# Two last V tiles cut otherwise, and a result whose halves lie on two partition quadrants of one PSUM bank

## The chip, the cores and the metric

One core of one Trainium2 chip. The metric is the device time of one execution in microseconds (us), as the median of several executions; the profile is of one execution. "Span" is the profile's own length, some 1.8 us shorter than the device time. The rounds of the experiments ran on three chips; each time is compared with the kernel before of the same rounds.

## The reference, cut to what matters

A decode step of a parallel block: attention of 4 batches and 32 heads over a cache of 8192 positions, plus a SwiGLU branch, plus the input. The caches K and V are 268 MB each and are read once.

```python
q = (xn @ wq) ...                                         # B=4, H=32, Dh=128
scores = einsum("bhqd,bhkd->bhqk", q, k_cache) * Dh**-0.5  # Sk = 8192
o = einsum("bhqk,bhkd->bhqd", softmax(scores), v_cache)
return x + o.reshape(B, 1, H*Dh) @ wo + (silu(xn @ w_gate) * (xn @ w_up)) @ w_down   # 4 x 512
```

## The kernel before

K and V come in 64 tiles of 4 MB each (128 partitions of 32 KB, 128 tokens of 128 values), all issued on one queue into five buffers. VectorE turns a K tile in eight transposes, TensorE (PE) multiplies it with q, two tiles later the V tile is multiplied with the weights. The last V tile is handled token by token (`pv_last`), in parts, so that little work is left after the last bytes. The output projection of a head is two matmuls of 256 columns, one for each half of the result, collected in two PSUM banks.

```python
def wo_mm(i):                                  # output projection of head i, summed up in PSUM
    for half in range(2):
        mm(yo_ps[half][0:B, :], otn[:, i, :],
           wo_t[0][:, i * D + half * DH:i * D + (half + 1) * DH], start=False)
# ... (in the loop over tiles)
    load_v(nv, (32, 32, 32, 16, 16) if nv == NT - 1 else (32,) * 4 if nv == NT - 2 else (T,))
# ...
    if npv == NT - 1:                          # the last V tile
        xps = x_tile()
        pv_last(xps, range(T // 2))
        fin_2(H // HT - 1, xps, nb=B - 1, start=False)   # the other three batches
        pv_last(xps, range(T // 2, T))
        fin_3(H // HT - 1, xps)                # divides: otn of the last two heads
# ...
    if bv % 2 == 0:
        row_sums(npv // 2)                     # a PE sum, and a reciprocal on VectorE that waits for it
# ... (after the loop)
res = [persist.tile([B, DH], dt.bfloat16, name=f"res{j}") for j in range(2)]
nc.vector.tensor_copy(out=res[0][:], in_=yo_ps[0][0:B, :])
nc.sync.dma_start(out=out_flat[:, 0:DH], in_=res[0][:])
nc.scalar.copy(out=res[1][:], in_=yo_ps[1][0:B, :])
nc.scalar.dma_start(out=out_flat[:, DH:D], in_=res[1][:])
```

## Time and profile before

| | before |
|---|---|
| device time | 1288.93 us, median of 3 (1288.82 to 1289.40) |
| span | 1287.1 us |
| HBM read | 550.77 MB, 428 GB/s |
| last V part landed | 1282.67 us |
| first of the last 59 P·V matmuls | 1266.04 us |
| from the last store's issue to the end | 2.10 us |

The page gives the shares of the whole span; a change of the tail is read from the chain and the timeline of the last 30 us (start, length, engine, line, operation, and in brackets the idle time before it and what ended that).

```profile
1254.35 0.18 DVE L328 RECIPROCAL rcp<-mps 128x4 f32<-128x4 f32 x1 [8.48 <-PE mps L76]
1254.45 9.11 DVE L277 STREAM_TRANSPOSE kt<-slot 128x1024 uint32<-128x1024 uint32 x8
```

The last K tile landed at 1253.35 by the records, but its transposes stand behind a reciprocal on VectorE that waits for PE.

### The profile page before, as it was taken

How to read it: one execution, taken by the hardware profiler on the slowest of the kernel's cores; microseconds unless marked ns; L12 is line 12 of the kernel's file. 1: busy time of each engine (PE TensorE's matmuls, PEld its weight loads, DVE VectorE, ACT ScalarE, POOL GpSimd, SP SyncE). 2: the span in 40 equal slices, each digit the busy share in tenths (PEclk: the TensorE clock that was granted, in tenths of full speed). 3: DMA queues.
4: the chain of work that ended last, by engine and by line, in shares of the span. 5: the costliest groups of instructions: out<-in, count | busy, mean ns of one | idle time of the engine just before them, and what ended most of it. 6: DMA issues, size and time to landing. Idle time of an engine off the chain costs nothing.

```text
span 1287.1 us, 11189 instructions
## 1 busy us (share of the span) xinstructions
PE 1083.1 (84%) x4778; PEld 430.3 (33%) x4778; DVE 738.1 (57%) x951; ACT 39.7 (3%) x87; POOL 5.3 (0%) x13
## 2 busy tenths in 40 slices
PE   4888888888888798897997888888887988978788
PEld 1334333333333333332333333333333333333334
DVE  6663556546556556466556566465465465573544
ACT  1000000000000000000000000000000000000000
POOL 1000000000000000000000000000000000000000
PEclk9898898998989999898998989989899898989899
DMA  9999999999999999999999999999999999999997
GB/s 407 427 430 435 437 425 437 429 436 431 432 435 428 436 432 433 431 432 435 431 435 428 434 432 431 436 431 433 430 434 431 437 430 432 433 431 427 433 434 304
DMA packets 21529, 551.49 MB, mean 428 GB/s; under 512 B 2268, under 2 KB 2792, under 8 KB 3944
## 3 DMA queue, kind: packets, MB, share of 16 engines
q1 hardware_dynamic: 21464, 550.78, 99.4%
q8 instruction: 37, 0.61, 0.2%
q14 instruction: 12, 0.10, 0.0%
q10 hardware_dynamic: 16, 0.01, 0.0%
HBM read 550.77 MB, written 0.00 MB: 428 GB/s over the span
## 4 chain that ended last, share of the span: by engine, by line
DMA 50%; PE 31%; DVE 14%; issue 5%; ACT 1%; SPq 0%; DVEq 0%
DMA slot<-in_A_k_cache_dram 44%; PE oacc L76 17%; PE sps L76 12%; DVE kt L277 11%; DMA slot<-in_A_v_cache_dram 6%; PE mps L76 1%; DVE ptz L318 1%; DVE o L356 1%; PE xps L76 1%; DVE o_sb L354 1%; ACT o_sb L353 0%; PE mps L299 0%; DVE otn L377 0%; PE yo_ps L76 0%; DVE rcp L328 0%
## 5 line engine op out<-in xcount | busy, mean ns | idle before, releaser
L76 PE MATMUL sps<-kt,zq 128*128 128x512 bf16 x2048 | 578.3, 421 | 145.2 <-DVE kt L277 128.7
L277 DVE STREAM_TRANSPOSE kt<-slot 128x1024 uint32<-128x1024 uint32 x512 | 587.6, 1210 | 90.4 <-DMA slot<-in_A_k_cache_dram 89.5
L76 PE MATMUL oacc<-slot,ptz 128*8 128x512 bf16 x2016 | 450.4, 379 | 0.4 <-DMA slot<-in_A_v_cache_dram 0.4
L76 PEld LDWEIGHTS <-zq 128*128 128x128 bf16 x2048 | 212.0, 104 | 496.1 <-issue 317.0
L76 PEld LDWEIGHTS <-ptz 128*8 128x8 bf16 x2016 | 177.5, 92 | 258.1 <-issue 27.8
L328 DVE RECIPROCAL rcp<-mps 128x4 f32<-128x4 f32 x32 | 5.9, 183 | 281.9 <-PE mps L76 281.9
L354 DVE TENSOR_TENSOR o_sb<-o_sb,rowu 128x512 f32<-128x512 f32 x16 | 11.1, 693 | 89.2 <-ACT o_sb L353 89.0
L76 PE MATMUL xps<-rowy,o 128*32 128x4 f32 (+1 forms) x228 | 13.5, 205 | 37.3 <-DVE o L356 37.3
L293 DVE TENSOR_REDUCE mx<-sps 128x1 f32<-128x512 f32 x32 | 22.1, 692 | 18.5 <-PE sps L76 18.5
L76 PEld LDWEIGHTS xps<-rowy,o 128*32 128x32 f32 (+1 forms) x228 | 12.1, 154 | 44.9 <-DVE o L356 44.9
L268 DVE COPY zq<-qt 32x8 bf16<-32x8 bf16 x128 | 21.3, 166 | 1.3
L302 DVE TENSOR_REDUCE nm<-mps 128x4 f32<-128x64 f32 x32 | 7.2, 225 | 24.0 <-PE mps L299 24.0
L356 DVE TENSOR_REDUCE o<-o_sb 128x128 f32<-128x512 f32 x16 | 16.3, 1020 | 0.5
L76 PEld LDWEIGHTS mps<-rowb,rs 128*128 128x128 f32 x64 | 9.5, 186 | 13.8 <-issue 13.8
L76 PEld LDWEIGHTS <-slot 128*128 128x128 bf16 x272 | 11.7, 126 | 3.5 <-DVE slot L188 2.6
L76 PE MATMUL mps<-rowb,rs 128*128 128x4 f32 x64 | 12.3, 263 | 0.0
L353 ACT COPY o_sb<-oacc 128x512 f32<-128x512 f32 x16 | 9.4, 586 | 76.8 <-PE oacc L76 76.8
L377 DVE TENSOR_TENSOR otn<-xps,rcp 32x16 bf16<-32x16 f32 x28 | 4.8, 170 | 11.7 <-PE xps L76 10.3
L299 PE MATMUL mps<-ident_f,mx 128*128 128x128 f32 x32 | 10.3, 323 | 0.8 <-DVE mx L293 0.8
L299 PEld LDWEIGHTS mps<-ident_f,mx 128*128 128x128 f32 x32 | 4.3, 133 | 14.7 <-DVE mx L293 14.2
L170 PE MATMUL xps<-ident,kt 4*128 4x4 bf16 x4 | 0.3, 173 | 10.1 <-DVE kt L165 10.1
L76 PE MATMUL yo_ps<-slot,otn 128*4 128x256 bf16 x64 | 8.2, 281 | 0.3 <-DVE otn L366 0.3
(150 smaller groups left out, 148.5 us busy)
## 6 DMA issues: line engine op xcount, KB each, us to landing
slot<-in_A_k_cache_dram SPq DMA_DIRECT2D x64, 4096.0 KB, 39.2
slot<-in_A_v_cache_dram SPq DMA_DIRECT2D x62, 4096.0 KB, 36.8
slot<-in_A_v_cache_dram SPq DMA_DIRECT2D x7, 1024.0 KB, 22.3
slot<-in_A_wq_dram SPq DMA_DIRECT2D x1, 4096.0 KB, 12.3
slot<-in_A_wo_dram SPq DMA_DIRECT2D x1, 3584.0 KB, 40.2
slot<-in_B_w_gate_dram SPq DMA_DIRECT2D x1, 1792.0 KB, 31.9
slot<-in_B_w_up_dram SPq DMA_DIRECT2D x1, 1792.0 KB, 35.8
slot<-in_B_w_down_dram SPq DMA_DIRECT2D x1, 1792.0 KB, 30.9
```

Of the source, the lines that this page charges most:

```text
L76: nc.tensor.matmul(out_ap, lhsT=lhsT, rhs=rhs, start=start, stop=True, skip_group_check=True, **kw)
L268: nc.vector.tensor_copy(out=zq[gr % 2][a * QB:(a + 1) * QB, :, :, XO + a * QB].rearrange("p b (j r) -> p r j b", r=2), in_=qt[a * QB:(a + ...
L277: nc.vector.transpose(out=kt[:].bitcast(dt.uint32).rearrange("p (j t r) -> p t j r", j=2, r=QB), in_=src.rearrange("p (t j r) -> p t j r", ...
L293: nc.vector.reduce_max(out=mx[:], in_=s_ps[gr][:], axis=AX.X)
L299: nc.tensor.matmul(mps[:, 0:P], lhsT=nmx.pop(gr)[:, 0:1].to_broadcast([P, P]), rhs=ident_f[:, :], is_transpose=True, start=True, stop=True ...
L302: nc.vector.tensor_reduce(out=nm[:], in_=by_row(mps[:, 0:P]), axis=AX.XY, op=ALU.max, negate=True)
L318: nc.vector.transpose(out=t_[y * HP:(y + 1) * HP, :, y, :, :].rearrange("p s u x -> p s (u x)"), in_=p_[y * HP:(y + 1) * HP, :].rearrange( ...
L328: nc.vector.reciprocal(out=rcp[j][:, :, 2 * bp:2 * bp + 2], in_=mps[:, P:P + B].rearrange("p (y b) -> p y b", y=HT))
L353: nc.scalar.copy(out=o_sb[:].rearrange("p u d -> p (u d)"), in_=o_acc[j % 2][:])
L354: nc.vector.tensor_tensor(out=o_sb[:], in0=o_sb[:], in1=rowu[:].unsqueeze(2).to_broadcast([P, NV, Dh]), op=ALU.mult)
L356: nc.vector.reduce_sum(out=o1[:], in_=o_sb[:].rearrange("p u d -> p d u"), axis=AX.X)
L377: nc.vector.tensor_tensor(out=otn[q0:q1, blk * 4:blk * 4 + 4, :], in0=xps[q0:q1], in1=r_[q0:q1, y, :].unsqueeze(1).to_broadcast([QB, 4, B] ...
```

## The change

The intent: let the two matmuls of a head run side by side (each half of the result on its own partition quadrant), share the rounding between two engines, and leave 8 tokens, not 16, to multiply after the last landing.

```diff
-    psY = ... bufs=2                      +    psY = ... bufs=1
-    yo_ps = [psY.tile([B, DH], dt.float32, name="yo_ps") for _ in range(2)]
+    yo_ps = psY.tile([2 * QB, DH], dt.float32, name="yo_ps")          # QB = 32
+    nc.vector.memset(yo_ps[:], 0.0)
+    def yo_mm(lhsT, rhs, start):
+        for a in range(2):
+            mm(yo_ps[a * QB:a * QB + B, :], lhsT, rhs[:, a * DH:(a + 1) * DH], start=start)
 ...
-            load_v(nv, (32, 32, 32, 16, 16) if nv == NT - 1 else (32,) * 4 if nv == NT - 2 else (T,))
+            load_v(nv, (64, 32, 16, 8, 8) if nv == NT - 1 else (64, 64) if nv == NT - 2 else (T,))
 ...
-    (the two roundings and two stores shown above)
+    res = persist.tile([2 * QB, DH], dt.bfloat16, name="res")
+    nc.scalar.copy(out=res[:, DH // 2:DH], in_=yo_ps[:, DH // 2:DH])
+    nc.vector.tensor_copy(out=res[:, 0:DH // 2], in_=yo_ps[:, 0:DH // 2])
+    nc.sync.dma_start(out=out_flat[:, 0:DH], in_=res[0:B, :])
+    nc.scalar.dma_start(out=out_flat[:, DH:D], in_=res[QB:QB + B, :])
```

(The two other users of `yo_ps` call `yo_mm`.)

## The prediction

> **What bounds the kernel now.** I read the page first: slices, the chain that ended last, the DMA issues. Then I read the stretch after 1270 us by windows, the chain again in order of time, the timeline, and when each transfer was issued and landed. Lines of the page:
>
> ```profile
> span 1287.1 us, 11189 instructions
> PE 1083.1 (84%) x4778; PEld 430.3 (33%) x4778; DVE 738.1 (57%) x951; ACT 39.7 (3%) x87; POOL 5.3 (0%) x13
> DMA  9999999999999999999999999999999999999997
> HBM read 550.77 MB, written 0.00 MB: 428 GB/s over the span
> ```
>
> The DMA row is 9 in every slice but the last: the kernel streams 551 MB of K and V and nothing else matters as long as the stream never pauses. The packet records say the same: a 32 KB packet takes 1213 ns nearly everywhere, one behind the other, and I found no pause after the first microseconds. So a change can only win in the head, in the stream's length, or in what follows the last landing. This one touches the tail and one memset in the head. Windows of the tail (us, busy of PE, PEld, DVE, ACT, POOL, granted clock, DMA share, GB/s):
>
> ```profile
> 1270.00:1275.00 5.00, 5.00 (x29) 2.17 (x28) 0.00 (x0) 0.00 (x0) 0.00 (x0) 1.00 1.00 418
> 1275.00:1277.00 2.00, 2.00 (x11) 0.83 (x10) 0.00 (x0) 0.00 (x0) 0.00 (x0) 1.00 0.57 242
> 1279.00:1281.00 2.00, 1.51 (x52) 1.42 (x49) 1.48 (x2) 0.00 (x0) 0.00 (x0) 1.00 0.51 203
> 1281.00:1283.00 2.00, 1.52 (x57) 1.43 (x54) 0.00 (x0) 0.00 (x0) 0.00 (x0) 0.56 0.14 55
> ```
>
> From 1275 us about half of the DMA capacity is idle: some of the 16 engines have finished, the slower ones work through the last parts until about 1282.4. The chain in order of time (start, length, what):
>
> ```profile
> 1265.54 17.13 DMA slot<-in_A_v_cache_dram
> 1282.67 0.05 issue
> 1282.71 0.60 PE xps L76 x16
> 1283.34 0.18 DVE otn L366
> 1283.56 1.03 PE yo_ps L76 x4
> 1284.61 0.36 ACT res L458
> ```
>
> So the last V part lands at 1282.67. Sixteen small matmuls, the division, four output matmuls and one rounding follow, then the stores:
>
> ```profile
> 1280.81 1.42 PE L76 MATMUL xps<-ptz,slot 128*128 128x2 bf16 x48
> 1284.40 0.41 DVE L456 CAST res<-yo_ps 4x256 bf16<-4x256 f32 x1 [0.89 <-PE yo_ps L76]
> 1284.84 0.35 SPq L457 DMA_DIRECT2D out_dram<-res  x1
> 1285.00 0.28 ACTq L459 DMA_DIRECT2D out_dram<-res  x1
> ```
>
> From the last store's issue at 1285.00 to the end at 1287.10 are 2.10 us; from the last V landing to the end, 4.43 us. That is all this change can work on, 0.34% of the span, so 2% is out of reach unless it starts a stall.
>
> **What the Trainium skill says.** "TensorE: Matmul & The Clock Gate", section "Part 3: Packing small matmuls", says that matmuls on different tiles of the array run at the same time. The trace agrees: in the head, 32 query matmuls of 512 columns over four column strips took 3.61 us, so 0.11 us each, where the same shape into one strip (the P·V matmuls, in the tail 59 in 12.06 us) takes 0.20 us at twice the granted clock. "PSUM — Partial Sum Buffer", section "PSUM bank collisions raise a hardware error", says that two engines may not access one bank in one quadrant at once, not even two reads. The trace of before has no such pair; the changed program, where both roundings read both quadrants, does, and its instruction list orders them. "VectorE: DVE Perf Modes", section "The TRN2 errata", gives a PSUM copy 172 + N cycles at 1.2 GHz on ScalarE and 120 + N at 0.96 GHz on VectorE: 357 and 392 ns for N = 256; the trace has 362 and 412. "DMA: Bandwidth & Descriptors", section "Anatomy of one DMA", puts a DMA's fixed cost at about 2.0 us, mostly the receipt; the 2.10 us here fits, and the change leaves it.
>
> **The change part by part.**
>
> *Parts of the last two V tiles.* Before: four parts of 32 tokens, then 32, 32, 32, 16, 16. After: 64 and 64, then 64, 32, 16, 8, 8: seven transfers for nine. An engine's share of a part is 8 packets, one per partition. The packet records give 159 ns for 4 KB, 309 for 8 KB, 535 for 14 KB, 1213 for 32 KB: some 8 ns and 0.0368 ns per byte, so (estimates) 610 ns for 16 KB and 83 for 2 KB, less 3 ns of overlap each. Both tiles cost an engine 8 x (7 x 306 + 2 x 156) = 19.63 us before and 8 x (3 x 607 + 306 + 156 + 2 x 80) = 19.54 after: -0.09 us.
>
> What remains after the last landing: 8 tokens, not 16. 16 took 0.60 us; with a step of 0.028 us (0.60 less a latency of 0.17, over 15) 8 take 0.36: -0.23 us. This holds only if PE is there in time. It restarts at 1280.70, after the sum of the other three batches, and did 48 tokens in 1.42 us, so it is through token 119 near 1282.4, or a little after the fourth part (about 1282.0); the fifth lands at 1282.58. It waits, with 0.2 us to spare.
>
> *Output matmuls.* The halves go to partitions 0 to 3 and 32 to 35 of one bank, two column strips, so the two matmuls of a head can run side by side. Before: four in a row in 1.03 us. At the granted half clock 256 columns take 0.213 us (half of the 0.427 in which four 512-column matmuls passed in the head), and 1.03 - 3 x 0.213 = 0.39 is the first one's latency. After: 0.39 + 0.213 = 0.61: -0.42 us. The 60 earlier output matmuls also pair up, inside the stream, where it is worth nothing.
>
> *Rounding.* Both engines now take 128 of the 256 columns, on 64 partitions, so each instruction is shorter: by the formulas, shifted to what the trace has, 0.25 us on ScalarE and 0.28 on VectorE. But the built program makes VectorE's copy wait for ScalarE's: they are not side by side. And both stores need both copies. Before: last matmul to last store's issue 1285.00 - 1284.59 = 0.41 us. After: 0.02 + 0.25 + 0.04 + 0.28 + 0.03 = 0.62: +0.21 us. Run truly side by side they would give 0.33, so the ordering costs about 0.3 of the possible gain.
>
> *Head.* One memset of 64x256 on VectorE: half of the 485 ns of a 128x512 one, 0.25 us. It falls before a 1.68 us wait of VectorE for the first K tile. Nothing.
>
> Sum: -0.09 - 0.23 - 0.42 + 0.21 = -0.53 us. 1288.93 - 0.53 = 1288.4.
>
> **The rivals.**
> 1. *A coarse part starves PE.* Two parts of 64 land later than the first of four. In the records the first 32-token part landed at 1265.52; at 8 x 0.306 = 2.45 us a part, the halves land near 1267.9 and 1272.8. PE reaches that tile 27 matmuls of 0.204 us after 1266.04, at 1271.5, and its second half at 1274.8. The last tile's first 64 tokens land near 1277.7 (the records have 1277.76 for their second half), and PE wants them at 1278.16. Margins of 2.0 and 0.4 us. If I misjudge the second, the delay partly hides behind the 1280.57 restart; I give a loss above 0.3 us a 10% chance.
> 2. *The stream ends at another time.* In before, the last two issues waited for a transfer slot (1263.05 and 1265.54). After, only one waits, for a K load that landed at 1253.35. But no engine ran dry before, so nothing is won. If the slow engines' lag came out differently, the end could move by a microsecond either way; this, like the run-to-run spread of 1288.82 to 1289.40, is larger than what I predict, and makes most of the range.
> 3. *The column strips do not overlap* for four-row results. Then 0.42 us is lost and the change is about -0.1: 1288.8. The query matmuls speak against it.
> 4. *The two roundings run together.* Then -0.8: 1288.1. The wait in the built program speaks against it.
>
> **Range and chances.** Rivals 3 and 4 span 1288.1 to 1288.8; the spread and rival 2 add some 0.6 us either way: 1287.4 to 1289.2. Beyond 2% (26 us) nothing I can name reaches; faster 0.5%, slower 1% for a stall I have overlooked, same 98.5%.
>
> **What would show it.** The page should look the same but for the tail. Right: a last landing within 0.3 us of 1282.6, then 8 matmuls in about 0.36 us; four output matmuls in about 0.6; ScalarE's copy at 0.25 us, and VectorE's beginning only when it ends, at 0.28; both stores issued within 0.1 us of each other, some 3.9 us or less between landing and end. Wrong: four output matmuls still near 1.0 us; copies that overlap; PE waiting for V before 1278, or arriving after the last landing; a landing more than 0.5 us away from 1282.6, which would mean that the stream and not the tail made the difference.

## The result, and the profile after

| | before | after |
|---|---|---|
| device time, median (range, runs) | 1288.91 (1288.78 to 1289.40, 6) | 1289.18 (1288.56 to 1289.31, 6) |
| span of the profiled execution | 1287.1 | 1287.4 |
| ratio | | 1.0001, 95% interval 0.9988 to 1.0014 |

A ratio is the mean time of one kernel's runs over that of the other's of the same rounds, so not quite the ratio of the medians. Kernels are compared only within the same rounds. The time lies inside the predicted range, at its upper edge; the half microsecond of gain that was forecast is not there. The chain of the changed kernel in order of time:

```profile
1266.74 12.00 PE oacc L76 x59
...
1280.11 1.04 DVE o L361
1281.15 0.04 issue
1281.19 2.31 PE xps L76 x66
1283.51 0.02 issue
1283.53 0.18 DVE otn L371
1283.71 0.04 issue
1283.75 0.61 PE yo_ps L76 x4
1284.36 0.02 issue
1284.38 0.27 ACT res L461
1284.65 0.02 issue
1284.67 0.28 DVE res L462
```

Where the chain of before went through the landing of the last V part, this one has no transfer at all in its last 20 us: P·V matmuls, the sum of the other batches, 64 tokens in one go, the output. The timeline says the same of those 64 tokens: no wait in brackets.

```profile
1281.64 1.85 PE L76 MATMUL xps<-ptz,slot 128*128 128x2 bf16 x64
1283.75 0.59 PE L76 MATMUL yo_ps<-slot,otn 128*4 128x256 bf16 x4 [0.26 <-DVE otn L371]
1284.67 0.28 DVE L462 CAST res<-yo_ps 64x128 bf16<-64x128 f32 x1 [0.98 <-ACT res L461]
1284.98 0.35 SPq L463 DMA_DIRECT2D out_dram<-res  x1
1284.99 0.28 ACTq L464 DMA_DIRECT2D out_dram<-res  x1
```

The last V part had landed at 1282.47, when PE still had some 35 tokens to go. Term by term, from the two profiles:

| stretch | before | after | difference |
|---|---|---|---|
| start to the end of the last token matmul | 1283.30 | 1283.49 | +0.19 |
| division, to the first output matmul | 0.26 | 0.26 | 0 |
| output matmuls (with the step to the rounding left out) | 1.01 | 0.59 | -0.42 |
| last output matmul to the last store's issue | 0.43 | 0.65 | +0.22 |
| last store's issue to the end | 2.11 | 2.38 | +0.27 |
| sum (span) | 1287.11 | 1287.37 | +0.26 |

Two terms are as predicted. Two are not: the token matmuls end later and not earlier, and the close is 0.27 us longer.

### The profile page after: what moved, and what is told of

It is laid out like the page before. It is cut to its first block, busy times and chain, and to the rows that moved or that the text cites. A ratio compares the mean times of both kernels' runs of the same rounds, so it can differ in the third digit from the quotient of the medians.

```text
span 1287.4 us, 11188 instructions
## 1 busy us (share of the span) xinstructions
PE 1083.6 (84%) x4778; PEld 430.5 (33%) x4778; DVE 738.0 (57%) x952; ACT 39.5 (3%) x87; POOL 5.3 (0%) x13
## 4 chain that ended last, share of the span: by engine, by line
DMA 46%; PE 35%; DVE 13%; issue 4%; ACT 1%; SPq 0%; DVEq 0%
DMA slot<-in_A_k_cache_dram 43%; PE oacc L76 18%; PE sps L76 15%; DVE kt L282 10%; DMA slot<-in_A_v_cache_dram 3%; DVE o L361 1%; PE mps L76 1%; PE xps L76 1%; DVE ptz L323 1%; DVE o_sb L359 1%; ACT o_sb L358 1%; PE mps L304 0%; DVE otn L382 0%; DVE yfx L246 0%; PE yo_ps L76 0%
## 5 line engine op out<-in xcount | busy, mean ns | idle before, releaser
L76 PE MATMUL mps<-xnt_w,slot 128*128 128x4 bf16 x112 | 6.8, 199 | 0.3 <-DVE rcp L333 0.3
```

What stands on the lines that cost most here:

```text
L76: nc.tensor.matmul(out_ap, lhsT=lhsT, rhs=rhs, start=start, stop=True, skip_group_check=True, **kw)
```

## The experiments

Ten kernels ran; all gave correct results. **Theory A**, formed on these two profiles: in the changed kernel the granted clock is halved from 1236.7 to 1243.5 us, where before had it full; that stage's score matmuls took longer (28 of them 8.60 us in place of 7.82), and everything on PE after it is 0.63 us late (the last 59 P·V matmuls start at 1266.67 in place of 1266.04). The paired output matmuls, which leave PE idle earlier just before (16 of them in 1.04 us in place of 1.91), would be the cause. **Rival R**: such half-clock stretches come and go from execution to execution, whatever the kernel. **Rival P**: the new parts of the V tiles are the cause. The stage begins with ScalarE's copy of the last head pair but one; the next P·V matmuls and the last 59 follow. Timeline of the kernel before, then of the changed one:

```profile
1232.38 0.59 ACT L353 COPY o_sb<-oacc 128x512 f32<-128x512 f32 x1 [4.44 <-PE oacc L76]
1246.91 7.08 PE L76 MATMUL oacc<-slot,ptz 128*8 128x512 bf16 x32
1266.04 12.06 PE L76 MATMUL oacc<-slot,ptz 128*8 128x512 bf16 x59
```

```profile
1232.24 0.58 ACT L358 COPY o_sb<-oacc 128x512 f32<-128x512 f32 x1 [4.44 <-PE oacc L76]
1247.55 7.08 PE L76 MATMUL oacc<-slot,ptz 128*8 128x512 bf16 x32
1266.67 12.06 PE L76 MATMUL oacc<-slot,ptz 128*8 128x512 bf16 x59
```

**Both kernels again, unchanged.**

> The kernel before, unchanged, for a second trace and more spans. Theory A (pairing the output matmuls inside the stream lets the clock be halved late): no half clock between 1203 and 1281 us, the last 59 P.V matmuls start near 1266.0, span 1287.1. Rival R (such late dips come and go from execution to execution whatever the kernel): this second trace may show a dip between 1203 and 1270 and then its last P.V row starts 0.6 us later.

> The changed kernel, unchanged. Theory A: the half clock near 1237 to 1243 is there again, the last 59 P.V matmuls start near 1266.7, span 1287.4. Rival R: the dip is missing about as often as not; where it is missing the P.V row starts near 1266.0 and the span is some 0.6 us shorter (the one execution of 1288.56 us with a span of 1286.8 among six could be such a case).

**One half of the change at a time.** The parts alone:

```diff
 (the kernel before)
-    load_v(nv, (32, 32, 32, 16, 16) if nv == NT - 1 else (32,) * 4 if nv == NT - 2 else (T,))
+    load_v(nv, (64, 32, 16, 8, 8) if nv == NT - 1 else (64, 64) if nv == NT - 2 else (T,))
```

> Before with the new parts of the last two V tiles alone. Theory A: no dip, P.V row at 1266.0; last landing 1282.5, then 8 matmuls in about 0.36 us, the two stores on the old two roundings: last store issued at about 1284.7, span 1286.8 (0.3 less). Rival P (the new parts, not the output matmuls, make PE late): P.V row at 1266.7 and a span of 1287.1 or more.

The output alone:

```diff
 (the changed kernel)
-    load_v(nv, (64, 32, 16, 8, 8) if nv == NT - 1 else (64, 64) if nv == NT - 2 else (T,))
+    load_v(nv, (32, 32, 32, 16, 16) if nv == NT - 1 else (32,) * 4 if nv == NT - 2 else (T,))
```

> The changed kernel with the old parts of the last two V tiles. Theory A: the dip near 1237 is there, 16 output matmuls of that round in 1.04 us in place of 1.91, P.V row at 1266.7, last token matmuls end near 1283.5 (bound by PE, or by the landing at 1282.67 plus 0.6 = 1283.3), span 1287.3. Rival P: no dip, P.V row at 1266.0, span 1287.1 - 0.42 + 0.22 + 0.3 (stores) = 1287.2. The dip and the P.V row tell them apart, not the span.

What was measured, of the profiled execution of each (and the median of its five or six times); "P·V row" is the start of the last 59 P·V matmuls:

| | half clock near 1236 | P·V row | last landing | last token ends | to the store's issue | issue to end | median |
|---|---|---|---|---|---|---|---|
| before | none | 1266.04 | 1282.67 | 1283.30 | 1.70 | 2.11 | 1288.91 |
| before again | none | 1266.27 | 1282.69 | 1283.33 | 1.70 | 2.12 | 1288.93 |
| after | 1236.7, 6.8 us | 1266.67 | 1282.47 | 1283.49 | 1.50 | 2.38 | 1289.18 |
| after again | 1235.2, 6.8 us | 1267.03 | 1282.59 | 1283.63 | 1.50 | 2.39 | 1289.04 |
| parts alone | 1235.5, 3.4 us | 1267.09 | 1282.36 | 1283.69 | 1.70 | 2.23 | 1288.78 |
| output alone | 1235.7, 3.4 us | 1267.25 | 1282.61 | 1283.85 | 1.49 | 2.26 | 1288.99 |

Theory A falls as it stands: the parts alone, whose output matmuls are the old ones, has the half clock too. The granted clock of that kernel by windows (busy of PE, PEld, DVE, ACT, POOL, then clock, DMA share, GB/s):

```profile
1232.00:1236.00 4.00, 1.54 (x8) 0.68 (x6) 1.71 (x2) 0.58 (x1) 0.00 (x0) 0.94 1.01 434
1236.00:1240.00 4.00, 4.00 (x21) 2.26 (x21) 3.69 (x5) 0.00 (x0) 0.00 (x0) 0.63 0.95 410
```

And of the kernel before, for the same windows:

```profile
1232.00:1236.00 4.00, 1.55 (x13) 0.99 (x12) 2.48 (x4) 0.59 (x1) 0.00 (x0) 1.00 0.99 426
1236.00:1240.00 4.00, 2.88 (x18) 1.37 (x16) 3.97 (x5) 0.00 (x0) 0.00 (x0) 1.00 0.95 410
```

In both, PE works only 1.5 of the 4 us before, because it waits for the end of a head pair; whether the clock is cut after that differs. Rival P falls too, since the output alone has the old parts and the half clock. Rival R stands as far as it goes: later runs have the half clock in the kernel before (with a move) and lack it in a variant of the changed one. The Trainium skill, "TensorE: Matmul & The Clock Gate", section "What's actually happening", says that the activity window is about 3.4 us and free-running, not tied to the kernel's start; the stretches here, 3.4 and 6.8 us long and starting at 1235.2, 1235.5, 1235.7 or 1236.7, agree. That the window's phase decides is the page's account and fits; no run here set the phase.

Two things stay open. Both traces of the kernel before lack the half clock and both of the changed kernel have it, so it is not shown that the change leaves its chance as it was; its costly form, 6.8 us from 1236.7 to 1237.0 on, is in three traces, all with paired output matmuls. And the half clock near 1236 is not all that made PE late. From ScalarE's copy to the next P·V matmuls take 14.53 us without it, 14.74 where it starts between 1235.2 and 1235.7, and 15.31 in after. But in after again, the parts alone and the output alone, that copy itself began at 1233.17 to 1233.39, 0.8 to 1.0 us later than in before. PE was late there already; why, no run shows.

**Does PE set the end?** The table suggests theory B: the last token ends at the later of two times. Where PE does not wait for V it ends 16.6 us after the P·V row starts (16.60 in three of these four; 16.82 in after, where a half clock that began at 1281.1 stretched the sum of the other batches from 0.39 to 0.59 us). Where PE waits, it ends at the landing plus 0.64 us (16 tokens). In before the second is later by 0.7 us and in before again by 0.5; in the other four the first. Theory B's test takes the reciprocal out of VectorE's way, so that the last K tile is turned as soon as it is there:

```diff
             for g in range(NTG):
                 t_piece(i, g)
                 s_piece(i, g)
 ...
+            if i == NT - 1:
+                row_sums(NT // 2 - 2)
 ...
-            if bv % 2 == 0:
+            if bv % 2 == 0 and npv != NT - 4:
                 row_sums(npv // 2)
```

> The changed kernel, with the row sums of the pair before the last (and the reciprocal on VectorE that waits for PE) moved behind the last K tile's transposes, so that VectorE starts these when the tile lands (1253.3) and not when PE is through (1254.4 to 1255.7 so far). Theory B (PE and not the last landing sets the end of the changed kernel, so its smaller last part earns nothing): the last 59 P.V matmuls start near 1265.0, PE waits for the last part at 1282.5, the last token matmul ends near 1282.85, span 1286.7 to 1286.8, and the five times are near 1288.5 with a narrow spread. Rival (the landing sets the end already): last token matmul near 1283.5 and span 1287.4 as before.

> The kernel before with the same move. Theory B: the kernel before was bound by the landing at 1282.67 in a quiet execution, so nothing is won there: last token matmul at 1283.3, span 1287.1; only the late executions (1287.4 to 1287.6) should be gone. Rival: a gain of 0.3 us or more in the median.

Measured, changed kernel with the move: P·V row 1265.03, last landing 1282.43, last token ends 1282.85, span 1286.74, median 1288.58 (1288.52 to 1289.36), with the half clock at 1237.0 for 6.8 us. Kernel before with the move: P·V row 1265.09, landing 1282.49, last token ends 1283.13, span 1286.93, median 1288.81 (1288.71 to 1289.03), with the half clock at 1235.3. The kernel before without the move had a median of 1288.81 in the same rounds (1288.59 to 1289.57, 9 runs), so there the move won nothing, as expected. (Its landing came 0.17 us before that of the first trace, but so did that of its last K tile, at 1253.18: that is the execution's stream.) Both are as theory B has them, and neither minds the half clock. In the changed kernel with the move, PE now waits for the last part, with 8 tokens to do:

```profile
1253.30 9.13 DVE L282 STREAM_TRANSPOSE kt<-slot 128x1024 uint32<-128x1024 uint32 x8 [7.48 <-DMA slot<-in_A_k_cache_dram]
...
1282.48 0.37 PE L76 MATMUL xps<-ptz,slot 128*128 128x2 bf16 x8 [0.26 <-DMA slot<-in_A_v_cache_dram]
```

From landing to the last token 0.42 us with 8 tokens and 0.64 with 16: the smaller part is worth 0.22 us, where PE is in time. One execution of the five (1289.36) was late all the same; it has no trace, and why is open.

**The longer close.** In the table the last stretch is 2.11, 2.23, 2.26 and 2.38 us for neither, parts, output and both: two costs that add up. The records of semaphores split them. In before the last store lands at 1286.22, 1.21 us after its issue, and in after at 1286.41, 1.43 us after (the stores were issued 0.16 us apart in the one, together in the other; the one that lands last is ScalarE's in before and SyncE's in after). The rest, 0.89 and 0.96 us, is the closing sequence: SyncE checks the completion semaphores in turn, one each 0.063 us. With seven V transfers in place of nine the stores hold lower numbers, so that each has two checks more behind it. In before one check is left after the store that lands last; in after it is the other store, with two left. Of the 0.27 us, then, 0.21 are the later landing and 0.06 one more check. In the parts alone ScalarE's store lands last as in before, with three checks left: 0.13 us. Theory C says so; its test gives the changed kernel nine transfers again:

```diff
-    load_v(nv, (64, 32, 16, 8, 8) if nv == NT - 1 else (64, 64) if nv == NT - 2 else (T,))
+    load_v(nv, (64, 32, 16, 8, 8) if nv == NT - 1 else (32,) * 4 if nv == NT - 2 else (T,))
```

> The changed kernel with the last tile but one in four parts again: nine V transfers, as before. Theory C (the two transfers fewer move the stores to lower completion semaphores, and the closing sequence, which checks them in order, then has more left to check after the last store): from the last store's issue to the end 2.26 us in place of 2.38, two closing waits of 0.063 us fewer after the last store has landed; landing itself still 1.43 us after its issue. Rival (the longer close comes from elsewhere): 2.38 again.

Measured: 2.26 us, with the store still landing 1.43 us after its issue and 0.83 us from there to the end in place of 0.96, which is two checks fewer. Theory C holds. This run had no half clock near 1236; its P·V row began at 1266.40 and the last token ended at 1282.99, 16.59 later. Its span was 1286.8, its median 1288.53 (1288.29 to 1289.35).

**The roundings and the stores.** The changed kernel's two copies stand in a row, though they write disjoint columns. Theory D: the bank in common does that.

```diff
-    yo_ps = psY.tile([2 * QB, DH], dt.float32, name="yo_ps")
+    yo_ps = [psY.tile([2 * QB, DH], dt.float32, name="yo_ps") for _ in range(2)]
 ...
-            mm(yo_ps[a * QB:a * QB + B, :], lhsT, ...)
+            mm(yo_ps[a][a * QB:a * QB + B, :], lhsT, ...)
 ...
-    (two copies of 64x128 and two stores)
+    res = persist.tile([B, D], dt.bfloat16, name="res")
+    nc.scalar.copy(out=res[:, DH:D], in_=yo_ps[1][QB:QB + B, :])
+    nc.vector.tensor_copy(out=res[:, 0:DH], in_=yo_ps[0][0:B, :])
+    nc.sync.dma_start(out=out_flat[:, :], in_=res[:])
```

> The changed kernel with the two halves in two banks (still on two partition quadrants), each rounded whole by one engine into rows 0 to 3 of one tile, and one store of four rows for two. Theory D (the bank in common is what puts the roundings in a row, and two stores issued together delay each other by 0.2 us): the two copies overlap, 0.36 and 0.41 us, output matmuls still 0.6 us, the store issued 0.46 us after the last matmul in place of 0.63, landed 1.21 us after its issue in place of 1.43; from the last token matmul to the end 3.5 us in place of 3.88. Rival: the copies still in a row (0.8 us), or the store as slow as the pair.

```profile
1283.87 0.59 PE L76 MATMUL yo_ps<-slot,otn 128*4 128x256 bf16 x4 [0.26 <-DVE otn L370]
1284.49 0.41 DVE L461 CAST res<-yo_ps 4x256 bf16<-4x256 f32 x1 [0.68 <-PE yo_ps L76]
1284.52 0.36 ACT L460 CAST res<-yo_ps 4x256 bf16<-4x256 f32 x1 [5.06 <-PE yo_ps L76]
1284.96 0.34 SPq L462 DMA_DIRECT2D out_dram<-res  x1
```

The copies overlap, the output matmuls still pair, and the store is issued 0.51 us after the last matmul (0.46 expected, 0.65 in after). It lands 1.27 us after its issue (1.21 expected, 1.43 in after). From the last token to the end 3.65 us, not 3.88; 3.5 had been expected. Both copies write one result tile here as there, so it is not that tile that put them in a row. What they no longer share is the PSUM tile, its bank and its quadrants, all at once; that the bank alone decides is not shown. The median was 1288.41 (1288.06 to 1289.20); the profiled execution was one of the late ones (P·V row 1266.78, span 1287.3).

**All of it together.** The two-bank version with the moved row sums, once with seven V transfers, and once with ten, so that the store's semaphore is the last to be checked:

```diff
 (two banks, one store, row sums moved; the second kernel also)
-    load_v(nv, (64, 32, 16, 8, 8) if nv == NT - 1 else (64, 64) if nv == NT - 2 else (T,))
+    load_v(nv, (64, 32, 16, 8, 4, 4) if nv == NT - 1 else (32,) * 4 if nv == NT - 2 else (T,))
```

> The two-bank, one-store version together with the moved row sums, seven V transfers. Theory B and D together: P.V row at 1265.0, last landing 1282.45, last token matmul ends 1282.85, then 3.64 us to the end as in the two-bank run: span 1286.5, times near 1288.25, and fewer executions that are 0.6 us late. Rival: the parts do not add up (the end moves less than 0.2 us against the run with the moved row sums alone).

> The same with ten V transfers (four of 32 tokens, then 64, 32, 16, 8, 4, 4), so that the store takes the completion semaphore that the closing sequence checks last. Theory C: from the store's issue to the end 2.29 - 3 x 0.063 = 2.10 us; 4 tokens after the last landing in place of 8 save 0.1 us more: span 1286.2, times near 1287.95. Rival: the many small last parts are issued too late or land later (after 1282.7) and eat it.

| | P·V row | last landing | last token ends | issue to end | span | median (range of 5) |
|---|---|---|---|---|---|---|
| seven transfers | 1265.07 | 1282.47 | 1282.90 | 2.29 | 1286.5 | 1288.40 (1288.17 to 1288.44) |
| ten transfers | 1265.24 | 1282.75 | 1283.07 | 2.10 | 1286.5 | 1288.22 (1288.13 to 1288.30) |
| before, same rounds | | | | | | 1288.85 (1288.62 to 1289.27, 9 runs) |

The close went from 2.29 to 2.10 us, as theory C said to the hundredth. The ten-transfer landing was 0.28 us later than the seven-transfer one, and the expected span of 1286.2 was missed by 0.3. The last K tile, issued before these parts, landed 0.17 us later too (1253.39 and 1253.21 by the records), so that much is the execution's. From the K landing to the V landing are 29.36 us against 29.26: the small parts cost 0.10 us, as much as the 4 tokens fewer saved (0.32 us from the landing to the last token, in place of 0.42). All five times of each lie under all nine of before. The ten-transfer kernel is the best of all that ran: its median is 0.63 us under that of the kernel before. That is 0.05% (ratio 0.9995, interval 0.9981 to 1.0008), so it is "same".

## Why the prediction was right or wrong, point by point

- *What bounds the kernel, and that only the 4.43 us after the last landing count.* Half right. The stream has no pauses, and no run gained more than 0.63 us. But beside the stream ran a second path, PE and VectorE from the end of the last head pair but one onward, which in the one execution that I read ended 0.7 us ahead of the stream's. I took it for slack in general.
- *Seven transfers for nine, -0.09 us.* The landings by themselves do not show it: 1282.30 to 1282.69 with nine transfers, 1282.36 to 1282.59 with seven. Counted from the landing of the last K tile they do: 29.32 to 29.33 us in the five traces with nine, 29.25 to 29.26 in the six with seven. So -0.06 us: right, if a little small.
- *8 tokens for 16, -0.23 us, "It waits, with 0.2 us to spare".* This step failed. The worth of the smaller part was right (0.22 us by the two runs with the row sums moved). But PE's arrival was taken from a single trace, which turned out to be the earliest of all whose row sums stay in place: their P·V rows start anywhere from 1266.04 to 1267.25. The slack was 0.2 us and the spread 1.2 us. In after PE did not wait for the last part at all, which the prediction had named as a sign of being wrong; the last token ended 0.19 us later than in before, and from landing to end were 4.90 us, not 3.9.
- *Output matmuls, -0.42 us.* Right: 1.03 to 0.61 us in the chains of the two kernels. Rival 3 did not occur.
- *Roundings in a row, +0.21 us.* Right: 0.26 and 0.28 us long, +0.22 to the store's issue. Rival 4 did not occur, and the two-bank run shows what the ordering cost.
- *"The 2.10 us here fits, and the change leaves it."* This step failed, and its reading was wrong too. A store takes 1.21 us of it; 0.89 are the closing sequence. The figure that was held against it is from a section on transfers that GpSimd issues; these are issued by SyncE and ScalarE. The change added 0.27: of two stores issued together one landed 1.43 us after its issue in place of 1.21, and one more semaphore (0.06 us) was checked after it.
- *Rival 1, a coarse part starves PE.* Did not occur: no wait for V before 1278 in after. *Rival 2* was near the truth in saying that the run-to-run spread is larger than the effect, but put it in the stream, whose landings differ by 0.4 us, where the P·V rows differ by 1.2.
- *Sum.* -0.53 predicted and +0.26 in the profile. The difference of 0.79 us is 0.5 from PE's lateness and 0.27 from the close; the other terms agree to a few hundredths.
- *Range and chances.* The range held, and "same" was right, because the whole tail is 0.34% of the span. That 1289.18 lies inside, by 0.02 us, is luck: the forecast gain did not come, and the two steps that failed are 0.8 us together.

## What to carry to other kernels

Where two paths end within a fraction of a microsecond of each other, the slack of one trace is no number to build on: look at two or three executions before counting on it, and first shorten the path that varies. Two roundings "side by side" ran in a row on two column ranges of one PSUM tile, and side by side with a tile, and so a bank, for each; the built program's waits show this before anything runs. After the last store, its place among the completion semaphores and the company of a second store were worth 0.06 to 0.21 us here.

## What the Trainium skill lacked or had wrong

- "DMA: Bandwidth & Descriptors", section "Anatomy of one DMA", gives about 2.0 us as a DMA's fixed cost, for transfers that GpSimd issues; it has no such figure for SyncE and ScalarE. A 2 KB store issued from SyncE or ScalarE landed 1.20 and 1.21 us after its issue when the two were 0.16 us apart, and 1.43 us for the later to land of two issued within 0.01 us; one 4 KB store took 1.27 us.
- No page has the price of the order of completion semaphores at the close: 0.063 us for each one that is checked after the last store's (2.29 us from issue to end with three behind it, 2.10 with none).
- "PSUM — Partial Sum Buffer" says that two readers of one bank and quadrant collide. The built program keeps the two roundings apart; the page doesn't give the price of that: 0.65 us from the last matmul to the last store's issue, against 0.51 with two banks and one store.
- "TensorE: Matmul & The Clock Gate" explains that the window is free-running, and gives the run-to-run spread of this for a kernel's start. It has none for the end of a long kernel: the last P·V row starts between 1266.04 and 1267.25 us in the eight traces with the row sums in place, and a half clock near 1236 makes 0.2 us (where it starts by 1235.7) or 0.8 us (from 1236.7 on) of that.
